# Feed-forward tiles finished inside attention, one tile stored instead of two; value sums multiplied with their reciprocals by GpSimd

## The chip, the cores and the metric

The kernel runs on one core of a Trainium2 chip. The metric is the device time of one execution in microseconds; a kernel's time is the median of its runs. TensorE multiplies matrices (PE; its weight loads are PEld), VectorE (DVE), ScalarE (ACT) and GpSimd (POOL) work element by element, and SyncE (SP) issues most of the DMAs. Each engine takes its own instructions in order; engines wait for each other through semaphores. TensorE writes to PSUM, of which the kernel uses eight tiles of 128 x 512: two each of the names pa, pb, ps1 and ps2.

## What is computed

Sequence S = 2048, width D = 512, 32 heads of 16, window W = 256, feed-forward width F = 1792, all in float32:

```python
qkv = (x @ wqkv) ...                            # 32 heads
scores = einsum("bhqd,bhkd->bhqk", q, k) * Dh ** -0.5
mask = (i - j >= 0) & (i - j < W)
a = (softmax(where(mask, scores, -1e9)) @ v) @ wo
b = (silu(x @ w_gate) * (x @ w_up)) @ w_down
g = sigmoid((x * gate_w).sum(-1))
out = g * a + (1 - g) * b
```

## The kernel before

Every float32 operand of a product is split in a high part (cast to the multiplication's type) and a low part (the rest), and a product is the sum of three: high x high, high x low, low x high. `split` does it with one cast and one subtraction.

The kernel has three stages. In preparation the inputs are split and the first two groups of heads are projected. In attention, heads go in 8 groups g of 4, and a group takes 16 **steps** t of four **blocks** hd. A block issues one score product of the next group, of which VectorE takes the row maximum (`stage1`: scores into ps1, then an add of the mask and a reduction in one operation, with its accumulator read), and one score product of this group, transposed, of which ScalarE takes the exponential (`stage2`: scores into ps2, then `pt`); GpSimd zeroes what lies outside the window. Every fourth step, behind block 1, `av` multiplies the exponentials with the values into one tile pb and one ps2 (pa and ps1 at the end). `finish` adds the two on VectorE, transposes, takes reciprocals of the sums (`rc`), multiplies, transposes back, and stores to `od`; its pieces are spread over the four steps that follow, at the blocks that the main loop names.

Into the same blocks go other products, three pairs of matmuls in each: the projections of the groups 2 to 7, key `("p", g)`, and the feed-forward products x @ w_gate and x @ w_up of 13 of the 14 tiles f of 128 columns, keys `("f", f, 0)` and `("f", f, 1)`. `lanes` computes two 512-column chunks m at a time, each on half of the array's rows, in two **turns** of 12 yields (one step each): in the second turn the chunks swap row halves. Since the two halves of one sum must not be accumulated at once, the first matmul of the second turn waits for an instruction of the list `BEHIND` (exponentials in the order in which they are issued; in preparation also score reductions): the first one recorded after the last matmul of the first turn was issued (`mark`).

`unit(key, t)` takes a whole key in four steps, with the two halves hf of the sequence interleaved: turn 0 of hf 0 in pa, turn 0 of hf 1 in pb, turn 1 of hf 0, turn 1 of hf 1. A step or two later ScalarE copies the finished tiles to `ev` tiles in SBUF (five of them in a ring, `kept`). Feed-forward tiles are stored to DRAM (`raws`, gate and up apart), projections are split and rearranged (`stack`).

`prepare` splits the weights of a coming key and starts the load of the next. In the last group, tiles of w_down are loaded, and the output gate is computed.

In the feed-forward stage, `load_kept` brings a gate tile and an up tile back per (f, c), `hidden` takes Silu of the gate tile on ScalarE and multiplies on VectorE, `halved` splits, and `step` multiplies with w_down (L85 to L87). Tile f = 13 is computed there whole (L700). The attention output is multiplied with wo beside it, and `put` mixes and stores. `tile0` does the first tile's Silu and product at the border of the stages.

Of the kernel before, what the change touches and what calls it, by code (L numbers as in the profile page):

```python
# [16 lines left out]
P = 128  # L17
S, D, H, DH, W, F = 2048, 512, 32, 16, 256, 1792
NK = D // P
NB = S // P  # L20
# [13 lines left out]
def gated_mix(ctx, tc, xT, xn, wqk, wv, wo, wgu, wd, gw, out):  # L34
# [103 lines left out]
    early = [("f", f, i) for f in range(NF - 1) for i in range(2)]  # L138
    KEPT = {(f, i, c) for _, f, i in early for c in range(NCH)}
    UNITS = []  # L140
# [8 lines left out]

    WKEYS = list(UNITS)  # L150
    WKEYS += [("f", NF - 1, i) for i in range(2)]
# [22 lines left out]
    with ExitStack() as A:  # L174
# [151 lines left out]
        def av(g, c):  # L326


            AV[g, c] = (pp.tile([P, CH], F32, name="pb" if 4 * g + c + 1 < len(UNITS) else "pa"),
                        ps1.tile([P, CH], F32, name="ps1") if 4 * g + c + 1 >= 4 * (G - 1) else ps2.tile([P, CH], F32, name="ps2"))  # L330

            orders = [[4 * c + m for m in ms if 4 * c + m >= 0] for ms in ((0, 1, 2, -1, -2, 3), (0, 1, -1, 2, 3, -2))]
            for n, kbs in enumerate(zip(*orders)):
                for j in range(4):
                    for h, (o, kb) in enumerate(zip(HALVES, kbs)):
                        k0 = kb * P + 64 * h
                        q0, q1 = max(k0, c * CH), min(k0 + W + 64, c * CH + CH)
                        nc.tensor.matmul(AV[g, c][h][32 * j:32 * j + 32, q0 - c * CH:q1 - c * CH],  # L338
                                         VG[4 * g + kb // 4][o, kb % 4, 17 * j:17 * j + 32],
                                         PT[g, kb, j // 2][o, j % 2, q0 - kb * P:q1 - kb * P],  # L340
                                         start=n == 0, stop=n == len(orders[0]) - 1, skip_group_check=True)
# [3 lines left out]
        def finish(g, c):  # L345
# [18 lines left out]
            nc.vector.tensor_tensor(out=v[:, :, :DH], in0=v[:, :, :DH],  # L364
# [147 lines left out]
        def unit(key, t):  # L512


            later(t, 3, prepare)

            def done(hf):
                def copies(ps):
                    t0 = t + 3 + hf
                    places = [kept(), kept()]  # L520
                    for m in range(2):
                        later(t0, 2 * m if t0 < G * NB else 0, lambda m=m: nc.scalar.copy(places[m], ps[m]))  # L522
                    if key[0] == "f":
                        for m in range(2):
                            later(t0 + 1, 2, lambda m=m: nc.sync.dma_start(raws[key[1], key[2], 2 * hf + m], places[m]))
                        return
                    g = key[1]

                    def half(m):
                        if m == 0:  # L530
                            X[g, hf] = x_pair()
                        split_qk(g, hf, m, places[m])
                    t1 = t0 + 3 * hf
                    later(t1, 3, lambda: half(0))
                    later(t1 + 1, 1, lambda: half(1))
                    later(t1 + 1, 3, lambda: stack(g, hf))
                return copies
# [43 lines left out]
        def tile0_load():  # L581
            for i, place in enumerate(halves_of(halves_of(KT[1][1])[0])):
                GOT[ORDER[0], i, 0] = place.bitcast(F32)
                nc.sync.dma_start(GOT[ORDER[0], i, 0], raws[ORDER[0], i, 0])

        def tile0():
            (gt, up), sg = [GOT.pop((ORDER[0], i, 0)) for i in range(2)], kept()
            nc.scalar.activation(sg, gt, AF.Silu)
            nc.vector.tensor_tensor(out=sg, in0=up, in1=sg, op=ALU.mult)
            split(*TILE0, sg, nc.scalar, nc.vector)  # L590
# [7 lines left out]
        for t in range(G * NB + 1):  # L598
            g, i = divmod(t, NB)
            d, part = divmod(t, NSLOT)  # L600
            if part == 0:
                turns = unit(UNITS[d], t) if d < len(UNITS) else [iter(())] * NSLOT
            s1 = stage1(g + 1, i) if t < g7 else iter(())
            s2 = stage2(g, i) if t < G * NB else iter(())
            for hd in range(4):
# [5 lines left out]
                run(turns[part], 3)  # L611
# [20 lines left out]
    with ExitStack() as B:  # L632
        hp = B.enter_context(tc.tile_pool(name="hp", bufs=3, side="right"))
        got = B.enter_context(tc.tile_pool(name="got", bufs=4, side="right"))
# [50 lines left out]
        def load_kept(c, f):  # L685

            for i in range(2):
                GOT[f, i, c] = got.tile([P, CH], F32, name=f"got{i}")
                nc.sync.dma_start(GOT[f, i, c], raws[f, i, c])

        def hidden(c, f):
            gu = []
            for i, name in enumerate(("pa", "pb")):
                if (f, i, c) in KEPT:
                    gu.append(GOT.pop((f, i, c)))
                    continue
# [6 lines left out]
            nc.scalar.activation(sg, gu[0], AF.Silu)  # L703
            nc.vector.tensor_tensor(out=sg, in0=gu[1], in1=sg, op=ALU.mult)  # L704
# [46 lines left out]
        for _ in range(3):  # L751
# [65 lines left out]
```

## Time and profile before

| | |
|---|---|
| median of 3 runs | 822.22 us (821.8 to 822.39) |
| the profiled execution | span 821.5 us from its first to its last instruction |
| mean granted TensorE clock | 1.000 |
| HBM read, written | 61.08 MB, 45.61 MB |
| 104 stores `raws`, 102 + 2 loads of it | 256 KB each |
| 512 exponentials (L316) | 477 ns each |
| 512 score reductions (L277) | 539 ns each, and 140 for the accumulator's read |
| 128 copies of `ev` (L522) | 587 ns each |

The profiled execution's own time is its span; the span is 0.7 us under the median of the runs. In the lines quoted below, L12 is line 12 of the kernel before. A row of a timeline gives start and length in us, engine, line, operation, output <- inputs with shapes, how many of them, and in brackets the idle time of the engine before it and what ended it. A row of a group gives the busy time in all and the mean of one in ns after the first bar, and after the second the idle time before it and its releasers.

### The profile page before, as it was taken

What the parts mean: (1) busy time and instruction counts of PE and PEld (TensorE: products, weight loads), DVE (VectorE), ACT (ScalarE), POOL (GpSimd) and SP (SyncE); (2) the same over time, 40 slices, a digit from 0 to 9 for tenths busy, and PEclk for the clock granted to TensorE, in tenths of its full rate; (3) what the DMA queues carried; (4) which work ended last, traced back from release to release, by engine and by line L of the source; (5) the groups of instructions that cost most, each with busy time, mean ns of one, the idle gap of its engine ahead of it and who ended that gap; (6) DMA issues with size and microseconds to landing.
All of it is one profiled execution on the core that took longest, in us unless ns stands there. A gap on an engine that the chain in (4) does not pass through costs nothing.

```text
span 821.5 us, 21573 instructions
## 1 busy us (share of the span) xinstructions
PE 815.1 (99%) x8329; PEld 683.8 (83%) x8329; DVE 515.6 (63%) x1437; ACT 448.9 (55%) x936; POOL 351.8 (43%) x640
## 2 busy tenths in 40 slices
PE   8999999999999999999999999999999999999998
PEld 7888988888888888888888888888887888888886
DVE  6397677677667676677677667756567453443543
ACT  6422666666656666666666666656654433333341
POOL 7812555555546555645554655456511221011020
PEclk9999999999999999999999999999999999999999
DMA  8574534624534543552562463466698563383531
GB/s 294 164 206 150 154 121 125 191 94 146 166 128 125 161 146 117 152 170 101 144 193 102 126 191 125 160 207 201 210 325 267 182 197 110 131 244 107 178 125 51
DMA packets 67957, 133.26 MB, mean 162 GB/s; under 512 B 11600, under 2 KB 16336, under 8 KB 67856
## 3 DMA queue, kind: packets, MB, share of 16 engines
q1 hardware_dynamic: 63888, 118.00, 46.3%
q0 software_dynamic: 3968, 13.90, 4.6%
q8 instruction: 65, 1.06, 0.6%
q14 instruction: 36, 0.29, 0.1%
HBM read 61.08 MB, written 45.61 MB: 130 GB/s over the span
## 4 chain that ended last, share of the span: by engine, by line
PE 95%; DMA 2%; DVE 1%; ACT 1%; issue 1%; SPq 0%; DVEq 0%; ACTq 0%
PE pb L225 24%; PE pa L225 24%; PE pb L338 7%; PE ps L275 6%; PE ps L87 5%; PE ps L85 5%; PE ps L86 5%; PE ps L314 5%; PE pb L205 2%; PE pa L205 2%; PE pb L85 2%; PE pb L87 2%; PE pb L86 2%; PE ps L338 2%; DMA got<-raws 1%; PE pb L700 1%
## 5 line engine op out<-in xcount | busy, mean ns | idle before, releaser
L277 DVE CUSTOM_DVE_ANT_0 ps<-ps,mask 128x384 f32<-128x384 f32 (+2 forms) x512 | 271.6, 539 | 143.2 <-PE ps L314 66.7
L316 ACT ACTIVATE pt<-ps 128x384 f32<-128x384 f32 (+2 forms) x512 | 240.7, 477 | 114.9 <-PE ps L275 57.7
L318 POOL TENSOR_SCALAR_AFFINE_SELECT pt<-pt 128x256 f32<-128x256 f32 x256 | 107.4, 419 | 223.8 <-ACT pt L316 220.4
L314 PE MATMUL ps<-q,k 64*128 64x384 f32 (+2 forms) x512 | 159.9, 329 | 0.0
L275 PE MATMUL ps<-k,q 63*128 63x384 f32 (+2 forms) x512 | 158.7, 330 | 0.0
L225 PE MATMUL pb<-xhi,wh 64*128 64x512 f32 x512 | 111.3, 394 | 0.0
L225 PE MATMUL pb<-xlo,wh 64*128 64x512 f32 x512 | 110.1, 391 | 0.0
L225 PE MATMUL pb<-xhi,wl 64*128 64x512 f32 x512 | 109.9, 392 | 0.0
L225 PE MATMUL pa<-xhi,wh 64*128 64x512 f32 x512 | 109.0, 394 | 0.0
L225 PE MATMUL pa<-xhi,wl 64*128 64x512 f32 x512 | 107.9, 391 | 0.0
L225 PE MATMUL pa<-xlo,wh 64*128 64x512 f32 x512 | 107.8, 391 | 0.0
L275 PEld LDWEIGHTS ps<-k,q 63*128 63x128 f32 x512 | 88.8, 185 | 16.9 <-issue 5.7
L321 POOL TENSOR_SCALAR_AFFINE_SELECT pt<-pt 128x256 f32<-128x256 f32 x224 | 98.7, 441 | 0.0
L314 PEld LDWEIGHTS ps<-q,k 64*128 64x128 f32 x512 | 89.9, 184 | 5.4 <-issue 0.8
L704 DVE TENSOR_TENSOR sg<-got,sg 128x512 f32<-128x512 f32 x51 | 45.1, 885 | 64.6 <-ACT sg L703 59.9
L338 PE MATMUL ps<-pt,vg 64*32 64x320 f32 (+4 forms) x1408 | 75.0, 346 | 0.0
L338 PE MATMUL pb<-pt,vg 64*32 64x320 f32 (+3 forms) x1360 | 73.9, 350 | 0.0
L277 DVE DVE_READ_ACCUMULATOR2_ANT mx<- 128x1 f32 x512 | 71.9, 140 | 0.0
L338 PEld LDWEIGHTS pb<-pt,vg 64*32 64x32 f32 x1360 | 46.4, 106 | 28.3 <-ACT pt L316 9.9
L225 PEld LDWEIGHTS pb<-xhi,wh 64*128 64x128 f32 x512 | 56.6, 185 | 7.9 <-ACT ev L522 0.3
L225 PEld LDWEIGHTS pb<-xhi,wl 64*128 64x128 f32 x512 | 56.5, 184 | 6.7
L225 PEld LDWEIGHTS pa<-xhi,wl 64*128 64x128 f32 x512 | 54.7, 184 | 7.4
(159 smaller groups left out, 1576.6 us busy)
## 6 DMA issues: line engine op xcount, KB each, us to landing
raws<-ev SPq DMA_DIRECT2D x104, 256.0 KB
got<-raws SPq DMA_DIRECT2D x102, 256.0 KB
od<-o POOLq DMA_DIRECT2D x32, 256.0 KB, 2.6
raw<-wgu SPq DMA_DIRECT2D x28, 256.0 KB
q<-xhi SPq DMA_DIRECT2D x56, 128.0 KB
k<-xhi SPq DMA_DIRECT2D x56, 128.0 KB
vd<-vs POOLq DMA_DIRECT2D x8, 672.0 KB, 5.1
vg<-vd SPq DMA_DIRECT2D x32, 168.0 KB
```

What stands on the lines that cost most here:

```text
L85: nc.tensor.matmul(ps, lh, rh, start=start and i == 0, stop=False, skip_group_check=skip)
L86: nc.tensor.matmul(ps, lh, rl, start=False, stop=False, skip_group_check=skip)
L87: nc.tensor.matmul(ps, ll, rh, start=False, stop=stop and i == n - 1, skip_group_check=skip)
L225: mm = nc.tensor.matmul(ps[me], w[r], x[r], start=not second and i == 0, stop=bool(second) and i == n - 1)
L275: nc.tensor.matmul(ps[:, :n], QT[g % 2][pr][r, q0:q0 + P], KT[g % 2][pr][r, k0:k0 + n], start=True, stop=True)
L277: mx = nc.vector.tensor_tensor_reduce(out=ps[:, :n], in0=ps[:, :n], in1=mask[:, 3 * P - n:], scale=1.0, scalar=NEG, op0=ALU.add, op1=ALU.m ...
L314: nc.tensor.matmul(ps[:, :n], KT[g % 2][pr][r, k0:k0 + P], QT[g % 2][pr][r, k0:k0 + n], start=True, stop=True)
L316: BEHIND.append(nc.scalar.activation(pt[:, j, :n], ps[:, :n], AF.Exp, scale=SCALE))
L318: nc.gpsimd.affine_select(out=pt[:, :, :P], in_=pt[:, :, :P], pattern=[[0, 2], [1, P]], compare_op=ALU.is_ge, fill=0.0, base=0, channel_mu ...
L321: nc.gpsimd.affine_select(out=pt[:, :, 2 * P:], in_=pt[:, :, 2 * P:], pattern=[[0, 2], [-1, P]], compare_op=ALU.is_ge, fill=0.0, base=-1, ...
L338: nc.tensor.matmul(AV[g, c][h][32 * j:32 * j + 32, q0 - c * CH:q1 - c * CH], VG[4 * g + kb // 4][o, kb % 4, 17 * j:17 * j + 32], PT[g, kb, ...
L704: nc.vector.tensor_tensor(out=sg, in0=gu[1], in1=sg, op=ALU.mult)
```

## The change

Instead of whole keys in four steps, `TURNS` lists pairs (key, half of the sequence), and `unit(n)` takes one pair in two steps: turn 0, then turn 1, in pa for even n and pb for odd n. For each tile f and half hf the gate product comes first (pa) and the up product next (pb). When the gate sum is done, ScalarE takes tanh of its half into an `ev` tile and VectorE multiplies (tanh + 1) with the sum; when the up sum is done, VectorE multiplies with one half and with the sum. That is silu(gate) x up, since silu(z) = z (1 + tanh(z / 2)) / 2. One tile per (f, chunk) is stored (`kept_h`), and the feed-forward stage only loads and splits it; the tile f = 13 uses the same formula there. Weights are prepared two steps ahead of a key's first turn. In `finish`, the product with the reciprocals is done by GpSimd. The pool of loaded tiles has eight places of one tile instead of four places of two names, and six loads are issued ahead instead of three pairs.

```diff
+    KEPT = {(f, c) for f in range(NF - 1) for c in range(NCH)}
+    tiles = iter([[(("f", f, i), hf) for i in range(2)] for f in range(NF - 1) for hf in range(2)])
+    TURNS = []
     for g in range(2, G):
-        UNITS += early[:2] + [("p", g)] + early[2:3]
-        early = early[3:]
-    UNITS += early
-    raws = dram.tile([NF - 1, 2, NCH, P, CH], F32, name="raws")
+        for n in range(4):
+            TURNS += [(("p", g), hf) for hf in range(2)] if n == 2 - g % 2 else next(tiles)
+    for two in tiles:
+        TURNS += two
...
+    kept_h = dram.tile([NF - 1, NCH, P, CH], F32, name="kept_h")
...
             nc.vector.reciprocal(rc, v[:, :, DH])
-            nc.vector.tensor_tensor(out=v[:, :, :DH], in0=v[:, :, :DH],
+            nc.gpsimd.tensor_tensor(out=v[:, :, :DH], in0=v[:, :, :DH],
                                     in1=rc[:, :, None].to_broadcast([P, CH // 32, DH]), op=ALU.mult)
...
-        def unit(key, t):
-            later(t, 3, prepare)
...
-            (a0, a1), (b0, b1) = (lanes(pp, name, [products(key, 2 * hf + m) for m in range(2)], done(hf))
-                                  for hf, name in enumerate(("pa", "pb")))
-            return [a0, b0, a1, b1]
+        for key in KEYS[1:-1]:
+            later(FIRST[key] - 2, 1, prepare)
...
+        def gate_half(t, f, hf):
+            def done(ps):
+                def tanh(m):
+                    SIL[f, hf, m] = kept()
+                    nc.scalar.activation(SIL[f, hf, m], ps[m], AF.Tanh, scale=0.5)
+                def product(m):
+                    nc.vector.scalar_tensor_tensor(SIL[f, hf, m], SIL[f, hf, m], 1.0, ps[m], op0=ALU.add, op1=ALU.mult)
+                for m in range(2):
+                    later(t + 2 + m, 0, lambda m=m: tanh(m))
+                    later(t + 2 + m, 3 - m, lambda m=m: product(m))
+            return done
+        def up_half(t, f, hf):
+            def done(ps):
+                hs = [SIL.pop((f, hf, m)) for m in range(2)]
+                def product(m):
+                    nc.vector.scalar_tensor_tensor(hs[m], hs[m], 0.5, ps[m], op0=ALU.mult, op1=ALU.mult)
+                for m in range(2):
+                    later(t + 2, 3 * m if t + 2 < G * NB else 0, lambda m=m: product(m))
+                    later(t + 3, 2, lambda m=m: nc.sync.dma_start(kept_h[f, 2 * hf + m], hs[m]))
+            return done
...
+        def unit(n):
+            t, (key, hf) = 2 * n, TURNS[n]
+            done = group_half(t, key[1], hf) if key[0] == "p" else (gate_half, up_half)[key[2]](t, key[1], hf)
+            return lanes(pp, ("pa", "pb")[n % 2], [products(key, 2 * hf + m) for m in range(2)], done)
...
-            if part == 0:
-                turns = unit(UNITS[d], t) if d < len(UNITS) else [iter(())] * NSLOT
+            if t % 2 == 0:
+                turns = unit(t // 2) if t < G * NB else [iter(())] * 2
...
-                run(turns[part], 3)
+                run(turns[t % 2], 3)
...
         def hidden(c, f):
+            if (f, c) in KEPT:
+                return GOT.pop((f, c))
...
-            nc.scalar.activation(sg, gu[0], AF.Silu)
-            nc.vector.tensor_tensor(out=sg, in0=gu[1], in1=sg, op=ALU.mult)
+            nc.scalar.activation(sg, gu[0], AF.Tanh, scale=0.5)
+            nc.vector.scalar_tensor_tensor(sg, sg, 1.0, gu[0], op0=ALU.add, op1=ALU.mult)
+            nc.vector.scalar_tensor_tensor(sg, sg, 0.5, gu[1], op0=ALU.mult, op1=ALU.mult)
             return sg
```

On TensorE, this is the border of a second turn in the kernel before, in attention; xhi, xlo, wh and wl are the high and low parts of x and of a weight tile, and what a row waits for stands in brackets (Activation is ScalarE):

```order
L225 MATMUL pa<-xlo_72,wh 128x512
L225 MATMUL pa<-xhi_73,wl 128x512
L225 MATMUL pa<-xhi_71,wl 128x512
L275 MATMUL ps_2440<-k_92,q_90 128x384 [waits DVE_49]
L314 MATMUL ps_2444<-q_358,k_360 128x384 [waits Activation_49]
L225 MATMUL pb<-xhi_77,wh 128x512
L225 MATMUL pb<-xhi_75,wh 128x512
L225 MATMUL pb<-xlo_78,wh 128x512
```

And the border of a second turn in the changed kernel:

```order
L229 MATMUL pa<-xlo_78,wh 128x512
L229 MATMUL pa<-xhi_75,wl 128x512
L229 MATMUL pa<-xhi_77,wl 128x512
L279 MATMUL ps_2308<-k_92,q_90 128x256 [waits DVE_49]
L318 MATMUL ps_2312<-q_358,k_360 128x384 [waits Activation_49]
L229 MATMUL pa<-xhi_77,wh 128x512 [waits Activation_49]
L229 MATMUL pa<-xhi_75,wh 128x512
L229 MATMUL pa<-xlo_78,wh 128x512
```

Before, the turn ahead is that of another tile (pa, then pb), and the second turn's first row waits for nothing. Now the same tile pa goes on, and its first row waits for ScalarE; by `mark` that is the exponential of the scores in the row just ahead (L318).

On VectorE, this is the last step of four and the first of the next in the kernel before, up to the sum of the value products (L355); `mx` rows are the score reductions with their accumulators' reads:

```order
L367 STREAM_TRANSPOSE o_1342<-o_1341 128x512
L277 ISA ps_2470,mx<-ps_2470,mask 128x384 [waits PE_49]
L277 ISA mx 128x1
L277 ISA ps_2484,mx<-ps_2484,mask 128x384 [waits PE_49]
L277 ISA mx 128x1
L277 ISA ps_2500,mx<-ps_2500,mask 128x384 [waits PE_49]
L277 ISA mx 128x1
L277 ISA ps_2516,mx<-ps_2516,mask 128x384 [waits PE_49]
L277 ISA mx 128x1
```

And the same place in the changed kernel, up to the up product (L541) that empties the tile pb which the value products take next:

```order
L371 STREAM_TRANSPOSE o_1342<-o_1341 128x512 [waits Pool_49]
L281 ISA ps_2466,mx<-ps_2466,mask 128x384 [waits PE_49]
L281 ISA mx 128x1
L529 SCALAR_TENSOR_TENSOR ev<-ev,pa 128x512 [waits DMAHW5_49,Activation_49]
L281 ISA ps_2480,mx<-ps_2480,mask 128x384 [waits PE_49]
L281 ISA mx 128x1
L281 ISA ps_2494,mx<-ps_2494,mask 128x384 [waits PE_49]
L281 ISA mx 128x1
L541 SCALAR_TENSOR_TENSOR ev<-ev,pb 128x512
```

Two products with PSUM operands stand among the reductions, and the transpose now waits for GpSimd. Ahead of these rows stands the reduction of the same block as the transpose.

More of the change, by code (lines that the diff above doesn't have):

```diff
@@ new lines, in group_half, with done, half @@
+        def group_half(t, g, hf):
+            t0 = t + 2 + (not hf)
+            def done(ps):
+                places = [kept(), kept()]
+                for m in range(2):
+                    later(t0, 2 * m, lambda m=m: nc.scalar.copy(places[m], ps[m]))
+                def half(m):
+                    if m == 0:
+                        X[g, hf] = x_pair()
+                    split_qk(g, hf, m, places[m])
+                first = t0 + 3 * hf
+                later(first, 3, lambda: half(0))
+                later(first + 1, 1, lambda: half(1))
+                later(max(first + 1, (g - 1) * NB) if hf else first + 1, 3, lambda: stack(g, hf))
+            return done
@@ L581, in tile0_load @@
         def tile0_load():
-            for i, place in enumerate(halves_of(halves_of(KT[1][1])[0])):
-                GOT[ORDER[0], i, 0] = place.bitcast(F32)
-                nc.sync.dma_start(GOT[ORDER[0], i, 0], raws[ORDER[0], i, 0])
+            GOT[ORDER[0], 0] = halves_of(halves_of(KT[1][1])[0])[0].bitcast(F32)
+            nc.sync.dma_start(GOT[ORDER[0], 0], kept_h[ORDER[0], 0])
         def tile0():
[L587 to L590, printed above, removed]
+            split(*TILE0, GOT.pop((ORDER[0], 0)), nc.scalar, nc.vector)
         later(g7 + NB - 4, 1, tile0_load)
@@ L633, in gated_mix @@
         hp = B.enter_context(tc.tile_pool(name="hp", bufs=3, side="right"))
[L634 removed]
+        got = B.enter_context(tc.tile_pool(name="got", bufs=8, side="right"))
         bp = B.enter_context(tc.tile_pool(name="bp", bufs=2))
@@ L750, in gated_mix @@
         loads = [(c, ORDER[n]) for c, n in seq if n != 1 and c + n]
-        for _ in range(3):
+        for _ in range(6):
             load_kept(*loads.pop(0))
```

41 lines of the change are left out of this document (9 added, 32 removed).

## The prediction

> **What bounds the kernel now.** I read the page's head and its busy times first, then the chain of work that ended last, then the windows by stage, and last the timeline of one stretch.
>
> ```profile
> span 821.5 us, 21573 instructions
> ...
> PE 815.1 (99%) x8329; PEld 683.8 (83%) x8329; DVE 515.6 (63%) x1437; ACT 448.9 (55%) x936; POOL 351.8 (43%) x640
> ...
> PE 95%; DMA 2%; DVE 1%; ACT 1%; issue 1%; SPq 0%; DVEq 0%; ACTq 0%
> ```
>
> TensorE is busy for 815.1 of 821.5 us and holds 95% of the chain. Nobody else sets the end: VectorE works 63% of the span, ScalarE 55%, GpSimd 43%. The stages are read one by one (columns: stretch, its length, then busy time of PE, PEld, DVE, ACT, POOL, granted clock, DMA share, GB/s): preparation up to 80.7, the 128 steps of attention up to 598, the feed-forward stage after it. The last row, from a finer answer, is the very end.
>
> ```profile
> 0.00:80.70 80.70, 78.53 (x530) 64.52 (x532) 52.39 (x155) 32.25 (x57) 40.34 (x50) 1.00 0.68 207
> 80.70:598.00 517.30, 517.25 (x6799) 438.36 (x6804) 357.32 (x1136) 330.25 (x730) 282.92 (x568) 1.00 0.48 151
> 598.00:821.50 223.50, 219.33 (x1019) 180.95 (x1003) 105.91 (x146) 86.44 (x151) 28.54 (x22) 1.00 0.54 173
> ```
>
> ```profile
> 815.00:821.50 6.50, 2.68 (x15) 2.17 (x13) 2.35 (x4) 0.00 (x0) 0.00 (x0) 0.96 0.43 161
> ```
>
> Preparation, with 2.17 us of standing, is not touched by the change. In attention TensorE is shown standing for 0.05 us; VectorE is busy 357 of 517 us. In the feed-forward stage TensorE stands 4.17 us, and 3.82 of these lie at the very end, behind the last products and the store. So whatever is taken off VectorE, ScalarE or the queues is worth under a microsecond, and whatever makes TensorE wait costs its full length. The question is only whether the change makes it wait.
>
> **The wait that the change adds.** Two chunks of a product are summed side by side, each on half of the array's rows, and swap the halves after the first of two turns; the first matmul of the second turn waits for the first exponential (or score reduction) recorded after the first turn's end. Before, another tile's turn stood between the two, so four exponentials had passed; the second turn's first row carries no wait. Now the second turn follows directly, and the exponential it must wait for is the one whose scores stand in the row just ahead of it (first pair of fences in the section on the change). 64 units of two turns make 64 such waits. Matmuls start in order, so all of TensorE's work stands behind each: the turn's 24 products, the next scores, and through them ScalarE and VectorE. What one wait costs is read from the same place in the trace of before:
>
> ```profile
> 301.19 0.34 PE L275 MATMUL ps<-k,q 63*128 63x384 f32 x1
> ...
> 301.20 0.33 PE L314 MATMUL ps<-q,k 64*128 64x384 f32 x1
> 301.37 0.39 PE L225 MATMUL pa<-xhi,wh 64*128 64x512 f32 x2
> ...
> 301.60 0.49 ACT L316 ACTIVATE pt<-ps 128x384 f32<-128x384 f32 x1 [0.37 <-PE ps L314]
> ...
> 303.80 0.33 PE L314 MATMUL ps<-q,k 64*128 64x384 f32 x1
> ...
> 303.97 0.40 PE L225 MATMUL pb<-xhi,wh 64*128 64x512 f32 x2
> ...
> 304.27 0.49 ACT L316 ACTIVATE pt<-ps 128x384 f32<-128x384 f32 x1 [0.37 <-PE ps L275]
> ```
>
> From the scores' start to the exponential's end it is 301.60 + 0.49 - 301.20 = 0.89 us in one block and 304.27 + 0.49 - 303.80 = 0.96 in the other, on average 0.93. The turn's products started 0.17 after the scores, and now start after the 0.93. The restart has a price too:
>
> ```profile
> 623.27 0.68 DVE L70 TENSOR_TENSOR hl<-sg,hh 128x512 fp32r<-128x512 f32 x1
> ...
> 623.71 0.39 PE L86 MATMUL ps<-k,hh 128*128 128x512 f32 x1
> ...
> 624.00 0.19 PEld L87 LDWEIGHTS ps<-k,hl 128*128 128x128 f32 x1 [0.32 <-DVE hl L70]
> 624.00 0.50 PE L87 MATMUL ps<-k,hl 128*128 128x512 f32 x1
> ```
>
> This matmul waited for VectorE, whose write ended at 623.95; it starts 0.05 later, its weight load has waited with it, and it lasts 0.50 instead of the 0.39 of its neighbour. So 0.03 to wake (between nothing and 0.05) and 0.11 for the uncovered load: one wait costs 0.93 + 0.03 + 0.11 - 0.17 = **0.90 us**. Bounds: 0.89 - 0.17 = 0.72 with neither, 0.96 + 0.05 + 0.11 - 0.17 = 0.95 with all. Times 64: **57.6 us** (46.1 to 60.8). In the last eight units two scores go out ahead of the turn and the wait is for the first exponential, so I leave them at the same price.
>
> A page bears on the 0.11. The Trainium skill (TensorE: Matmul & The Clock Gate, Part 2, step 1) says that TensorE pulls a weight load ahead of matmuls in flight. By that the load would be over when the wait ends, and the sum would be 64 x 0.11 = 7 us less, some 875 us. The row at 624.00 speaks against it where the matmul waits on a semaphore: there the load waited too.
>
> **The other parts.** TensorE's matmuls are the same in number and size, in another order. Of the rest, these rows carry the prices (line, engine, operation | busy in all, mean ns):
>
> ```profile
> L70 POOL TENSOR_TENSOR wl<-raw,wh 128x512 fp32r<-128x512 f32 (+2 forms) x36 | 46.1, 1281 | 3.2 <-ACT wh L67 3.2
> L704 DVE TENSOR_TENSOR sg<-got,sg 128x512 f32<-128x512 f32 x51 | 45.1, 885 | 64.6 <-ACT sg L703 59.9 <-DMA got<-raws 4.7
> ...
> L522 ACT COPY ev<-pb 128x512 f32<-128x512 f32 x64 | 37.7, 590 | 0.5 <-PE pb L225 0.5
> ...
> L703 ACT ACTIVATE sg<-got 128x512 f32<-128x512 f32 x51 | 32.1, 629 | 4.6 <-DMA got<-raws 3.6 <-DVE hl L70 1.0
> ...
> L364 DVE TENSOR_TENSOR o<-o,rc 128x256 f32<-128x256 f32 x32 | 16.4, 511 | 1.1
> ...
> L675 DVE SCALAR_TENSOR_TENSOR k<-ps,igate,k 128x512 f32<-128x512 f32 x8 | 5.4, 742 | 0.0
> ...
> L588 ACT ACT_TABLE_LOAD x1 | 1.3, 1283 | 0.0
> ```
>
> And the transfers, from the page's list of DMA issues:
>
> ```profile
> raws<-ev SPq DMA_DIRECT2D x104, 256.0 KB
> got<-raws SPq DMA_DIRECT2D x102, 256.0 KB
> ```
>
> - Feed-forward stage: 51 Silu (32.1 us), 51 products (45.1 us), half of the 102 loads and one table load leave ScalarE, VectorE and the queues. TensorE's matmuls cover them all; only its own stands ahead of the end can go: 4.17 - 3.82 = 0.35, and the 0.32 at 624.00, which the busy time hides. I take -0.6 us (0 to -0.7). The one tile loaded goes straight to the split; with up to eight in flight it is not late where two tiles of each pair were not.
> - ScalarE in attention: 104 of the copies (0.59 each) go, 52 tanh come, for which the Silu row's 0.63 is nearest. Its load falls by 61 - 33 = 28 us; nothing waits longer.
> - GpSimd: 32 value products. Below, VectorE's 0.51; above, GpSimd's 1.28 for twice the elements, and half of it is 0.64, which I take. The next user, VectorE's second transpose, stands a whole step (four blocks) later, some 3.5 us, and the one long job that may stand ahead on GpSimd is a 1.28 us weight split: covered, 0 us. Without that cover each would delay VectorE by up to 1.3 us.
> - The halved stores and the weights' splits, now two steps apart instead of four, stay off the path: a split takes 0.6 + 1.3 us and its load waits behind nothing longer, against 2 x 3.5 us.
> - VectorE in attention gains 104 scalar-tensor-tensor products at 0.74 (77 us) and loses 16.4. On average it has room (357 of 517 us, then some 418 of 575), but it works in order, and the value sums need an accumulator that its up-product frees.
>
> The last is the second place at which TensorE can wait. The spacing of VectorE's jobs when they queue:
>
> ```profile
> 301.03 0.55 DVE L277 CUSTOM_DVE_ANT_0 ps<-ps,mask 128x384 f32<-128x384 f32 x1
> ...
> 301.56 0.57 DVE L277 CUSTOM_DVE_ANT_0 ps<-ps,mask 128x384 f32<-128x384 f32 x1
> ...
> 303.79 0.71 DVE L367 STREAM_TRANSPOSE o<-o 128x512 f32<-128x512 f32 x1
> ...
> 304.42 0.54 DVE L277 CUSTOM_DVE_ANT_0 ps<-ps,mask 128x384 f32<-128x384 f32 x1
> ...
> 306.87 0.51 ACT L316 ACTIVATE pt<-ps 128x384 f32<-128x384 f32 x1
> ...
> 307.05 0.40 PE L225 MATMUL pa<-xhi,wl 64*128 64x512 f32 x2
> ...
> 307.38 0.10 PEld L338 LDWEIGHTS pb<-pt,vg 64*32 64x32 f32 x1 [0.37 <-ACT pt L316]
> ```
>
> A reduction follows the one before after 0.53, a job follows a transpose after 0.63; a product of mean 0.74 I put at 0.67. Count from the start of the last step of four, whose block 0 now has the 0.90 wait; a block is 0.87 (three of them lie between the scores at 301.20 and those at 303.80). Block 1's scores start at 1.77 and reach VectorE 0.37 later (301.19 to 301.56), at 2.14. Then come in its order, up to the product that frees the accumulator, four reductions, a transpose and two products (second pair of fences): 4 x 0.53 + 0.63 + 2 x 0.67 = 4.09, end 6.23, some 0.07 for the write: 6.30. TensorE reaches the value sums after six blocks and the wait, 6 x 0.87 + 0.90 = 6.12. In the trace of before it waits there already, for an exponential that ends at 307.38; the last pair of products began at 307.05 and such pairs follow each other after 0.23, so that wait is worth 0.1. So 0.1 us more at 26 places: **3 us**; bounds 0, and 0.5 x 26 = 13 if the jobs take their whole 0.57, 0.71 and 0.74.
>
> **Sum:** 821.5 + 57.6 + 3 - 0.6 = 881.5 us for the profiled execution. The median of the runs, 822.22, lies 0.7 above its span, so the forecast is **882 us**. From the bounds: 822.2 + 46.1 + 0 - 0.7 = 868 to 822.2 + 60.8 + 13 - 0 = 896.
>
> **Rivals.**
> 1. *No wait, so not slower.* If the exponential named is one that is over already, as before, 822.2 - 0.6 = **821.6 us** is left, and the small gain counts as none. It turns on one point: whether at least one more block of products stands between the exponential's scores and the waiting matmul (0.93 of latency against a block of 0.87 brings the wait to about 0.1). The rows show none between them. Chance 0.04.
> 2. *VectorE becomes the bound of a round.* If its products run as slowly as the 885 ns of the row of L704, and GpSimd's product lands late besides, both tanh products and the accumulator come late: the chain above grows by some 0.2 x 2 for the products and 1.3 for the transpose, and 26 x 1.7 = 44 us come on top of 879: **923 us**; half of it 901. For it: VectorE is the next engine in load. Against: the 0.74 row reads PSUM as these do, and each wait lets VectorE catch up 0.9. Chance 0.06 for more than 896.
> 3. *The clock falls because TensorE stands often.* What the trace has of short idles:
>
> ```profile
> 8.00:10.00 2.00, 1.51 (x6) 0.86 (x6) 1.40 (x3) 1.80 (x3) 0.00 (x0) 1.00 0.92 197
> ```
>
> With 0.49 us idle in 2 us the granted clock stays 1.00; only behind the last 3.8 us it is 0.96. At 0.96 over attention's 517 us, 517 x 0.04 = 21 us come on top: **903 us**. Chance 0.03. The Trainium skill (TensorE: Matmul & The Clock Gate, Part 1, on PSUM-queue cycling) reports a kernel whose short idles between groups made the clock swing to half; 64 swings of one 3.4 us window would be 64 x 1.7 = 109 us by that page, an estimate, and some 990. The row at 8.00, with its idles at full clock, does not bear it out.
>
> **How the numbers follow.** Forecast 0.84 (within 866 to 896), and 0.03 for a smaller loss than the bounds allow; the rivals as given. The range 866 to 896 leaves out 0.16. A measurement of this kernel tells about 0.2% (1.6 us) from no change. Slower: 0.84 + 0.03 + 0.06 + 0.03 = 0.96; same 0.03 and faster 0.01, both out of rival 1.
>
> **What would show it.** In the profile after: TensorE's busy time stays near 815 while the span grows, or its weight loads show idle of some 0.5 to 0.8 us, 64 times, released by ScalarE's exponential at the turns' line; two steps of attention last 0.9 us longer; the clock row stays at 1.00; the feed-forward stage from its first matmul to the end is as long as before within 1 us; VectorE's idle behind scores grows. Wrong if these waits are absent or under 0.5 us each, if value sums wait for VectorE over 0.5 us each, or if the stage after attention changes by several us.

## The result and the profile after

The changed kernel takes 887.74 us, 1.0795 times the kernel before [1.0777, 1.0812]. One of its four executions, the profiled one, took 1682.09 us with a TensorE that was slow from preparation on, where the change does nothing (226 matmuls in the first 80.7 us, 530 before), while the others took 887.21 to 888.1. Measured a second time beside the first experiments it took 887.78 us; the profile below is from there, and its span lies 65.3 us above that of before (886.8 - 821.5). This is the head of the page after, with the chain of work that ended last:

```profile
span 886.8 us, 21259 instructions
...
PE 836.0 (94%) x8329; PEld 677.7 (76%) x8329; DVE 519.2 (59%) x1461; ACT 401.5 (45%) x831; POOL 362.7 (41%) x672
...
PE 90%; DVE 4%; ACT 4%; DMA 1%; issue 1%; SPq 0%; POOL 0%; DVEq 0%; ACTq 0%
```

TensorE has the same 8329 matmuls, but now it stands for 50.8 us of the span, where it stood 6.4 before, and each restart lengthens its busy time besides. ScalarE and VectorE, which had 1% of the chain each, have 4%. By stages (the same columns as before, the borders moved to the same places of the program):

```profile
0.00:80.70 80.70, 78.66 (x532) 65.20 (x534) 52.33 (x157) 32.57 (x58) 39.57 (x51) 1.00 0.66 207
80.70:664.20 583.50, 538.64 (x6797) 431.50 (x6801) 392.86 (x1207) 312.43 (x678) 295.54 (x600) 0.99 0.35 110
664.20:886.80 222.60, 218.73 (x1018) 180.98 (x995) 74.00 (x100) 56.48 (x96) 27.59 (x23) 1.00 0.36 114
```

All of the loss lies in attention: 583.5 us for the same work as 517.3, with the DMA share down from 0.48 to 0.35 and ScalarE's busy time down by 18 us. None of what was saved there is seen in the time. What TensorE and its weight loads waited for (us in total, times, longest):

```profile
PE pa L229 <- ACT pt L320: 19.3, 32, 0.6
PE pb L229 <- ACT pt L320: 17.8, 32, 0.7
PE pb L342 <- DVE ev L541: 6.3, 8, 2.1
PE pa L229 <- DVE ev L529: 1.4, 2, 1.3
...
PEld pa L229 <- ACT pt L320: 30.7, 32, 1.0
PEld pb L229 <- ACT pt L320: 29.8, 32, 1.1
PEld pb L342 <- DVE ev L541: 15.9, 24, 2.6
```

The 64 waits at the turns' line are there, released by the exponential, and 24 waits of the value sums for VectorE's up product. In the kernel before, the rows for PE hold none of these, and the value sums' weight loads wait for ScalarE:

```profile
PEld pb L338 <- ACT pt L316: 9.9, 27, 0.4
```

One of the 64 waits, in the timeline of the changed kernel:

```profile
328.93 0.33 PE L318 MATMUL ps<-q,k 64*128 64x384 f32 x1
...
329.35 0.49 ACT L320 ACTIVATE pt<-ps 128x384 f32<-128x384 f32 x1 [0.39 <-PE ps L279]
...
329.89 0.19 PEld L229 LDWEIGHTS pb<-xhi,wh 64*128 64x128 f32 x2 [1.00 <-ACT pt L320]
329.89 0.50 PE L229 MATMUL pb<-xhi,wh 64*128 64x512 f32 x2 [0.61 <-ACT pt L320]
...
330.23 0.40 PE L229 MATMUL pb<-xlo,wh 64*128 64x512 f32 x2
...
330.46 0.40 PE L229 MATMUL pb<-xhi,wl 64*128 64x512 f32 x2
```

The exponential ends 329.35 + 0.49 - 328.93 = 0.91 after its scores' start, the turn begins 0.05 later and not 0.17 after the scores, and the next pair of products follows after 0.34 and not after 0.23: 0.91 + 0.05 - 0.17 + 0.11 = 0.90 us. The weight load waited with its matmul, so the 0.11 is paid; the pull-ahead of which the Trainium skill speaks (TensorE: Matmul & The Clock Gate, Part 2, step 1) does not help here.

Where the 65.3 us lie is read from a marker. Near the end of the next to last group SP sends its last row of maxima (`q<-md`), behind 56 of the 64 second turns; the first matmul of the feed-forward stage ends attention. For the kernel before:

```profile
538.25 0.99 SPq L293 DMA_DIRECT2D q<-md  x2
...
L700 PE MATMUL pa<-xhi,wh x16: 389/389/497, 598.9 to 762.4; 128*128 128x512 f32 x16
```

For the changed kernel:

```profile
592.50 0.98 SPq L297 DMA_DIRECT2D q<-md  x2
...
L724 PE MATMUL pa<-xhi,wh x16: 389/389/496, 665.0 to 827.7; 128*128 128x512 f32 x16
```

Up to the marker 54.2 us are lost, in the last group 72.5 - 60.7 = 11.8, and the feed-forward stage, from its first matmul to the end, falls from 222.6 to 221.8 us.

### The profile page after: what moved, and what is told of

It is laid out like the page before. It is cut to its first block, busy times and chain, and to the rows that moved or that the text cites. A ratio compares the mean times of both kernels' runs of the same rounds, so it can differ in the third digit from the quotient of the medians.

```text
span 1680.3 us, 21259 instructions
## 1 busy us (share of the span) xinstructions
PE 1637.9 (97%) x8329; PEld 1069.0 (64%) x8329; DVE 534.3 (32%) x1461; ACT 408.2 (24%) x831; POOL 359.6 (21%) x672
## 2 busy tenths in 40 slices
DMA packets 52979, 105.97 MB, mean 63 GB/s; under 512 B 9936, under 2 KB 14672, under 8 KB 52880
## 4 chain that ended last, share of the span: by engine, by line
PE 98%; ACT 2%; issue 0%; DVE 0%; POOL 0%; DVEq 0%; POOLq 0%; ACTq 0%
PE pb L229 24%; PE pa L229 24%; PE ps L279 7%; PE ps L85 6%; PE ps L87 6%; PE ps L86 6%; PE pb L342 5%; PE ps L318 3%; PE ps L342 3%; PE pb L209 2%; PE pa L209 2%; PE pb L86 2%; ACT pt L320 2%; PE pb L87 2%; PE pb L85 2%; PE pa L724 1%
## 5 line engine op out<-in xcount | busy, mean ns | idle before, releaser
L279 PE MATMUL ps<-k,q 63*128 63x384 f32 (+2 forms) x512 | 251.6, 525 | 0.0
L318 PE MATMUL ps<-q,k 64*128 64x384 f32 (+2 forms) x512 | 250.2, 521 | 0.0
L229 PE MATMUL pb<-xhi,wh 64*128 64x512 f32 x512 | 181.5, 679 | 17.9 <-ACT pt L320 17.9
L229 PE MATMUL pa<-xhi,wh 64*128 64x512 f32 x512 | 179.9, 676 | 19.2 <-ACT pt L320 19.2
L229 PE MATMUL pb<-xhi,wl 64*128 64x512 f32 x512 | 181.9, 679 | 0.0
L229 PE MATMUL pa<-xhi,wl 64*128 64x512 f32 x512 | 180.2, 676 | 0.0
L229 PE MATMUL pa<-xlo,wh 64*128 64x512 f32 x512 | 180.1, 674 | 0.0
L229 PE MATMUL pb<-xlo,wh 64*128 64x512 f32 x512 | 179.8, 670 | 0.0
L318 PEld LDWEIGHTS ps<-q,k 64*128 64x128 f32 x512 | 143.0, 295 | 25.0 <-issue 12.9
L342 PE MATMUL pb<-pt,vg 64*32 64x320 f32 (+3 forms) x1360 | 142.1, 606 | 0.0
L229 PEld LDWEIGHTS pa<-xhi,wh 64*128 64x128 f32 x512 | 75.7, 277 | 70.9 <-ACT pt L320 42.7
```

What stands on the lines that cost most here:

```text
L229: mm = nc.tensor.matmul(ps[me], w[r], x[r], start=not second and i == 0, stop=bool(second) and i == n - 1)
L279: nc.tensor.matmul(ps[:, :n], QT[g % 2][pr][r, q0:q0 + P], KT[g % 2][pr][r, k0:k0 + n], start=True, stop=True)
L318: nc.tensor.matmul(ps[:, :n], KT[g % 2][pr][r, k0:k0 + P], QT[g % 2][pr][r, k0:k0 + n], start=True, stop=True)
```

## The experiments

Each was timed beside the kernel before, on the same chip as it (the kernel before took 822.1 to 822.4 us each time). Three theories were open. A: each second turn waits for an exponential just issued. B: products that stand on VectorE return PSUM tiles late, since its queue is in order. C: GpSimd's product, or another part of the change, costs time too.

**1. The changed kernel again.**

> The changed kernel once more, for a profile of a run that is not disturbed. Theory A (the second turn's wait): 64 waits of TensorE's weight loads for the exponential, 0.5 to 0.8 us of recorded idle each, 885 to 890 us in all, and the feed-forward stage as long as before. Theory B (VectorE's added load and order): the largest waits of TensorE are for VectorE, spread over all blocks. Theory C (GpSimd's product is late): VectorE's second transposes wait for GpSimd, over 1 us each.

887.78 us (ratio 1.0786 [1.077, 1.0803]); its profile is the one above.

**2. The kernel before, with the order of the turns alone.**

```diff
-            return [a0, b0, a1, b1]
+            return [a0, a1, b0, b1]
```

> The kernel before with one line changed: the four turns of a key in the order pa, pa, pb, pb instead of pa, pb, pa, pb. Nothing else of the change is in it. Theory A: 64 waits of 0.9 us, 822.3 + 57 = 879 us (868 to 884). Theory B and theory C: 822 us, since VectorE and GpSimd do what they did.

882.21 us (ratio 1.0727 [1.0712, 1.0742]): 59.8 us, 0.93 for each of the 64 waits. One line of order, which removes and adds no instruction, makes nine tenths of the loss. Its weight loads' waits at the turns:

```profile
PEld pa L225 <- ACT pt L316: 35.8, 32, 1.2
PEld pb L225 <- ACT pt L316: 30.3, 32, 1.1
```

**3. The changed kernel, with gate and up turns interleaved** over four steps as before, and everything that hangs on their ends moved along; only the core is shown.

```diff
+                turns = list(two) if part == 0 else [turns[0], two[0], turns[1], two[1]]
...
-                    later(t + 2, 3 * m if t + 2 < G * NB else 0, lambda m=m: product(m))
+                    later(t + 4, 3 * m if t + 4 < G * NB else 0, lambda m=m: product(m))
```

> The changed kernel with its gate and up turns interleaved again (gate, up, gate, up over four steps), and the evacuations and the pieces of the value sums' finish moved to fit; all operations are the changed kernel's. Theory A: the 64 waits are gone and 821 to 828 us are left. Theory B: still over 870 us. Theory C: still over 870 us, since GpSimd multiplies as in the changed kernel.

853.75 us (ratio 1.0378 [1.0364, 1.0392]), so A's expectation, 821 to 828, missed by over 25 us, and those of B and C, over 870, by over 16. The 64 waits are gone, but others have come:

```profile
PEld pb L229 <- DVE ev L542: 14.6, 25, 0.9
...
PEld pb L342 <- DVE ev L542: 13.3, 24, 1.5
...
PEld pa L229 <- DVE ev L530: 7.4, 5, 2.4
```

The timeline shows how: the product that frees a tile pb stands in VectorE's queue behind a reduction and the value sums' adding, and the next turn in pb is due before it has ended.

```profile
202.66 0.68 DVE L359 TENSOR_TENSOR o<-pb,o 128x512 f32<-128x512 f32 x1
...
203.27 0.56 DVE L281 CUSTOM_DVE_ANT_0 ps<-ps,mask 128x384 f32<-128x384 f32 x1
...
203.74 0.68 DVE L542 SCALAR_TENSOR_TENSOR ev<-ev,pb 128x512 f32<-128x512 f32 x1
...
204.47 0.49 PE L229 MATMUL pb<-xhi,wh 64*128 64x512 f32 x1 [0.36 <-DVE ev L542]
```

**4. The kernel before, with GpSimd's product alone.**

```diff
-            nc.vector.tensor_tensor(out=v[:, :, :DH], in0=v[:, :, :DH],
+            nc.gpsimd.tensor_tensor(out=v[:, :, :DH], in0=v[:, :, :DH],
```

> The kernel before with only the value sums' product moved to GpSimd. Theory A: within 1 us of 822.3. Theory B: the same or up to 1 us less. Theory C: slower by tens of us, and VectorE's second transposes wait for GpSimd.

822.23 us (ratio 0.9999 [0.999, 1.0008]). VectorE waits for it (`DVE o L367 <- POOL o L364`, 6.1 us at five places), and TensorE does not. For the product, C falls.

**5. Half the dose of the second run.**

```diff
-            return [a0, b0, a1, b1]
+            return [a0, a1, b0, b1] if t % 8 == 0 else [a0, b0, a1, b1]
```

> The kernel before, with the second turns put straight behind the first ones in every other unit of four steps only (32 of the 64 pairs); nothing else of the change. A (each of these turns waits for the exponential whose scores stand in the row just ahead, at a fixed price): half of the 59.8 us that all 64 cost, so 822.4 + 29.9 = 852.3 us, 850.5 to 854.5, and some 66 / 2 = 33 us of weight-load waits for the exponential at the turns, 32 times. Rival (the waits are a matter of the stage's balance: ScalarE or VectorE fall behind once for all, and recover where the order is loose): clearly other than half, below 845 or above 860 us.

852.99 us (ratio 1.0372 [1.0355, 1.0389]): 30.8 us for 32 waits, 0.96 each. The loss goes with the number of waits, as A says.

**6 and 7. The third run, with the products on VectorE one place earlier:** first the up products alone, then the gate's tanh and products too.

```diff
-                    later(t + 4, 3 * m if t + 4 < G * NB else 0, lambda m=m: product(m))
+                    later(t + 3 + m, 3 - 3 * m, lambda m=m: product(m))
```

```diff
-                    later(t + 3, m, lambda m=m: tanh(m))
-                    later(t + 3, m + 1, lambda m=m: product(m))
+                    later(t + 2 + m, 3 - 3 * m, lambda m=m: tanh(m))
+                    later(t + 3, m, lambda m=m: product(m))
```

> The changed kernel with its turns interleaved as before (853.75 us), and only the two products of each up pair moved ahead by one place: to the end of the step in which its second turn ends, and to the start of the next. B (the 31 us by which that kernel stands over the kernel before come from PSUM tiles that VectorE gives back one step too late, behind the value sums' adding in its queue): the waits of pb's turns and of the value sums for these products go, 14.6 and 13.3 us of weight-load waits, of which some 10 come back as the wait for the exponential that the kernel before has too; with the restarts 829 to 834 us, the gate products' 7 us still there. Rival (VectorE's whole load, or the clock, makes the 31 us): no more than 5 us go, 848 us or above.

> As the run with the up products moved, and the gate's tanh and products moved ahead by one place too (a tanh at the end of the step of the gate's second turn, the products in the two places behind). A with B: no turn waits for an exponential just issued, no PSUM tile comes back late, so the kernel before less the 0.9 us of the feed-forward stage: 821.5 us, 820 to 825. That would put all of the change's loss on the order in which the turns stand and the places at which products stand, and nothing on fewer stores, more GpSimd or the finished tiles themselves. Rival (VectorE's added work costs time wherever it stands): 828 us or above.

835.44 us (ratio 1.0162 [1.0146, 1.0177]) and 833.96 (1.0144 [1.0125, 1.0162]). The up products of 26 pairs at another place of the same queue take 18.3 us away (the expectation, 829 to 834, is missed by 1.4), which bears out B and not VectorE's load. But the second of the two was expected at 821.5, and 12 us were still there: it is only 1.5 us below the first, and their intervals overlap. TensorE's waits for gate products (7.7 us in the sixth run) are gone in it, but its value sums wait 7.5 us for up products, which they did not in the sixth. By the same marker, 542.72 and 611.0, 4.5 of the 12 lie ahead of the last group and 7.6 in it. There VectorE and TensorE of the seventh run show:

```profile
554.60 2.53 DVE L586 SCALAR_TENSOR_TENSOR xhi<-xlo,xhi 128x512 f32<-128x512 f32 x1
...
557.38 0.43 DVE L69 CAST q<-ev 128x512 fp32r<-128x512 f32 x1 [0.24 <-DMA ev<-wd]
...
559.05 1.28 DVE L542 SCALAR_TENSOR_TENSOR ev<-ev,pb 128x512 f32<-128x512 f32 x2
```

```profile
559.79 0.45 PE L342 MATMUL pb<-pt,vg 64*32 64x320 f32 x1 [3.40 <-DVE ev L542]
```

The up products stand behind the output gate's blocks of xn (L586) and the pieces of w_down (L69). The row of L586 shows no wait for a transfer: it lasts 2.53 us, where the middle one of its 16 lasts 0.76, and why is not shown. It does not set the time, though. The chain that ended last (start, length, what) goes back to w_down's transfer, which SP issued behind its fetch of xn (L583); and that fetch waits for VectorE to be done with an earlier block:

```profile
551.74 0.56 DVE xhi L586 x2
...
552.32 0.33 SPq L583
...
552.70 4.65 DMA ev<-wd
...
557.38 0.44 DVE q L69
...
559.14 0.61 DVE ev L542
```

Other blocks of xn do wait for their own transfers, 5.6 us at two places. The kernel before has such waits of VectorE there too (8.3 us for xn at four places in its trace, 3.7 for w_down), but its copies out of PSUM stood on ScalarE. That is a new theory, D: the change put a reader of PSUM into a queue that waits for DMAs.

**8. The changed kernel, with the up products one place earlier.**

```diff
-                    later(t + 2, 3 * m if t + 2 < G * NB else 0, lambda m=m: product(m))
+                    later(t + 1 + m, 3 - 3 * m, lambda m=m: product(m))
```

> The changed kernel with the two products of each up pair one place earlier, nothing else; its 64 second turns still wait for the exponential. A with B: the value sums' 15.9 us of waits for these products go, and some 10 us come back as the wait for the exponential that the kernel before has there; 887.8 less 6 (4 to 8) = 882 us, 880 to 884, as the kernel before with this order of the turns alone (882.2). Rival (the 5.6 us between these two come from VectorE's load, or from the clock's fall late in the last group): 886 us or above, or the granted clock between 620 and 640 us as low as in the changed kernel.

883.43 us (ratio 1.0748 [1.0726, 1.0769]), 4.35 us less, within the expectation. Its marker stands at 587.74, 4.8 ahead of the changed kernel's: that is what late up products cost the value sums up to the last group. TensorE's seven waits for them there, 4.1 us, are gone, and the granted clock is 1.00 up to the marker in both. The 56 waits that are left cost 587.74 - 538.25 = 49.5, or 0.88 each. In the last group it is still 9.8 us over the kernel before, of which 8 x 0.88 = 7.0 are waits; the value sums' longest wait for L541, 2.2 us, is there, and so is a granted clock of 0.83 between 618 and 628 us. So the rival's lower clock is there too, with up products early or late, but it lies behind the marker and doesn't make the 4.8.

**9 and 12. The seventh run, with more time for the transfers:** in the ninth for xn and w_down, in the twelfth for xn alone (the edit of the first fence).

```diff
-            t = g7 - 4 + b // 2 * 2
+            t = g7 - 4 + b
...
-            later(t + 1, 2 + b % 2, lambda b=b: gate_block(b))
+            later(t + 2, 0, lambda b=b: gate_block(b))
```

```diff
-            later(t, 2, lambda: later(t + 1, 2, load_wd(f, piece, kept())))
+            later(t, 2, lambda: later(t + 2, 1, load_wd(f, piece, kept())))
```

> The run with interleaved turns and all products early (833.96 us), and in the last group the transfers that VectorE waits for get more time: the blocks of xn one a step and multiplied seven places after their fetch instead of five, the pieces of wd split seven places after theirs instead of four. D (what is left of the loss, 12 us ahead of the feed-forward stage, comes from VectorE waiting in its queue for xn and wd while the up products and with them the value sums of TensorE stand behind; 7.5 us of waits at four places and a clock of 0.83 for 10 us after the longest): most of it goes, 824 us, 822 to 828, and the granted clock between 550 and 610 us is 1.00 throughout. Rival (the transfers only come later, since SP issues them no earlier, or the waits move to other engines): 831 us or above.

> The run with interleaved turns and all products early (833.96 us), with the blocks of xn one a step and their longer lead, and nothing else: the pieces of wd and the weights at their old places. It parts the two transfers that VectorE waits for. If xn's alone hold TensorE up: 826 to 828 us, the last stage again 222.3 us from its first matmul to the end; if wd's alone do: 833 to 835 us; if both: between, some 830 us. It also says what moving the weights by one place did in the run before this (836.23 us, where six value sums wait 9.1 us for a copy behind it): if that was the whole of it, this run is below 832 us.

827.96 us (ratio 1.007 [1.0056, 1.0084]) and 827.76 (1.0074 [1.0061, 1.0087]): 6 us of the 12 go, so 827.96 lies at the edge of what was expected (824, 822 to 828), and the granted clock of the ninth is 1.00 as expected. In the twelfth run attention ends at 604.0 instead of 611.0, 6.3 of these 7 behind the marker (542.00). That bears out D, and moving xn's blocks alone is enough; but it doesn't part the two transfers, since both stand in SP's queue and the edit moves VectorE's blocks too. From 540 us on, VectorE waits 5.6 us for xn and 2.4 for w_down in the seventh run, and 0 and 7.7 in the twelfth. So the waits for transfers are no shorter in sum, only the value sums wait less behind them. Part of the 6 us is the clock, which falls to 0.63 for 4 us in the seventh run (last section) and stays at 1.00 in the twelfth. In the ninth attention ends at 602.2, but the late split of the last pieces makes the feed-forward stage 224.2 us instead of 222.3 (826.4 and 833.3 less the first matmul's time). The waits of the value sums for L542, 7.5 us in the seventh run (four, the longest 3.4), are gone in the ninth; in the twelfth they are

```profile
PE pb L342 <- DVE ev L542: 2.3, 3, 1.1
```

**10. The seventh run, with the value product on VectorE again** (the edit of the fourth run undone).

> The run with interleaved turns and all products early (833.96 us), and the value sums multiplied with their reciprocals by VectorE again. D: VectorE waits for transfers as before, so no change, 833 to 835 us. Rival (GpSimd's product costs after all once products stand on VectorE: VectorE's 3.8 us of waits for it in the last group, and the masks that stand in GpSimd's queue behind a product that waits 3.6 us for its reciprocals): 830 us or below.

836.51 us (ratio 1.0175 [1.0158, 1.0192]), 2.6 us more than the seventh run where no change was expected; the intervals just touch. GpSimd's product costs nothing here either, and where VectorE's queue holds TensorE up it seems to save a little.

**11. The twelfth run, with the weights split one place earlier.**

```diff
-            later(t if key[0] == "f" and key[2] else t - 1, 1, prepare)
+            later(t if key[0] == "f" and key[2] else t - 1, 0, prepare)
```

> Interleaved turns, all products early, the blocks of xn one a step with their longer lead as in the run before this (827.96 us), but the pieces of wd split at their old places, since the late split of the last ones made the feed-forward stage 2 us longer there (224.2 us from its first matmul to the end, against 222.3); and the weights split one place earlier, since seven turns wait 0.4 us for a weight half by GpSimd. D: the 222.3 us come back, the weights give up to 1 us, 825 us, 822 to 827; what the wd pieces' waits cost in VectorE's queue shows as 0 to 3 us more in the last group. Even at best this is the kernel before within 0.4 us, because fewer stores and GpSimd's product bring TensorE nothing. Rival (the finished tiles save something that the waits have hidden so far): below 820 us.

836.23 us (ratio 1.0162 [1.0144, 1.0179]), 8.5 us more than without the edit, where up to 1 us less was expected. The profiled execution, at a clock of 1.000, is 5.4 us longer than the twelfth run's (831.9 and 826.5); three of the five show a clock of 0.996 to 0.998 and are some 3 us longer still. The waits say why the 5.4:

```profile
PE pb L342 <- ACT ev L555: 9.1, 6, 2.2
```

In the timeline, the longest of the six:

```profile
446.45 0.62 ACT L67 CAST wh<-raw 128x512 fp32r<-128x512 f32 x1 [2.02 <-DMA raw<-wgu]
446.98 0.58 ACT L555 COPY ev<-pb 128x512 f32<-128x512 f32 x1
...
447.61 0.45 PE L342 MATMUL pb<-pt,vg 64*32 64x320 f32 x1 [2.23 <-ACT ev L555]
```

It is D on another engine: the weight split, moved ahead, waits 2.02 us in ScalarE's queue for its transfer, a projection's copy out of PSUM (L555) stands behind it, and the value sums wait for that tile. The rival, a saving that the waits had hidden, is not seen in any run: none is measurably below the kernel before.

## Why the prediction was right, and where its sizes were off

It forecast 882 us (866 to 896); measured were 887.74. Its own steps:

1. *What bounds the kernel.* That only what makes TensorE wait counts was borne out from both sides: 27 MB less traffic (133.26 to 105.97 in the pages' totals) and 47 us less work for ScalarE (448.9 to 401.5) bought 0.8 us at most (step 5), and one line of order cost 59.8 us.
2. *64 waits for the exponential just ahead, 0.90 us each, 57.6 us.* Right, in place, number and size: 0.90 in the timeline above, 0.93 and 0.96 by the doses in the kernel before, whose ScalarE has copies besides, and 0.88 by the marker of the eighth run, so some 56 us of the changed kernel's 65.
3. *VectorE's order makes value sums wait 0.1 us at 26 places, 3 us (0 to 13).* The mechanism was right, 24 places by the profile; the size was too small. The eighth run puts the part up to the last group at 4.8 us, 0.2 a place. One of its signs of being wrong was met, value sums that wait over 0.5 us each for VectorE: their weight loads wait 0.66 (15.9 us at 24 places). But in the kernel before they waited 0.37 for the exponential already (9.9 us at 27), so the change adds less than that sign counts.
4. *What the sum lacked* lies in the last group: 11.8 us lost there, against 7.0 of turn waits. The reading of VectorE's queue was made for a group with score reductions, and the last group has waits for transfers in it instead, for xn ahead of a gate product and for w_down ahead of an up product:

```profile
623.06 0.69 DVE L585 SCALAR_TENSOR_TENSOR xhi<-xlo,xhi 128x512 f32<-128x512 f32 x1 [2.64 <-DMA xlo<-xn]
...
624.42 0.49 PE L229 MATMUL pa<-xhi,wh 64*128 64x512 f32 x1 [1.25 <-DVE ev L529]
...
625.26 0.95 DVE L69 CAST q<-ev 128x512 fp32r<-128x512 f32 x1 [0.90 <-DMA ev<-wd]
...
627.46 0.68 DVE L541 SCALAR_TENSOR_TENSOR ev<-ev,pb 128x512 f32<-128x512 f32 x1
...
628.20 0.74 PE L342 MATMUL pb<-pt,vg 64*32 64x320 f32 x1 [2.14 <-DVE ev L541]
```

   Two standstills of 1.25 and 2.14 us, and behind them a lower clock (below). The four runs of this kernel have mean clocks of 1.000, 0.998, 0.996 and 0.996 and spans of 884.2, 885.4, 886.5 and 886.8, so by these four the clock makes some 2.6 of the 4.8 us that are left, and late products the other 2.2; both are estimates.
5. *The feed-forward stage, -0.6 us.* Measured -0.8. *ScalarE, stores, weight splits, GpSimd: 0.* Right by the fourth run for GpSimd, whose product took 0.62 us where 0.64 was taken; it is not covered everywhere (VectorE's second transposes wait 4.8 us for it, at five places), but TensorE does not wait there. For the others, TensorE shows no wait in the changed kernel. The loads were read less well: in attention ScalarE's busy time fell by 17.8 us and not 28, and VectorE's grew by 35.5 and not some 61; no term of the sum hangs on them.

Added up: 49.5 + 4.8 up to the marker, 7.0 + 2.6 + 2.2 in the last group, -0.8 behind it, 65.3 us. Since single executions of one kernel lie up to 4 us apart (the eighth run's spans go from 880.0 to 884.4), the smaller terms are good to 2 us or so.

The rivals: with no wait, 821.6, was refuted by the waits themselves. VectorE as the bound of every round did not come; its products took 0.68 us and not 0.885. The clock's fall over all of attention did not come either; it was confined to one place that the prediction had not named.

**What stays open.** The best order found here, 827.76, is still 5.6 us over the kernel before. 542.00 - 538.25 = 3.8 of them lie ahead of the last group. The weight loads of seven turns wait 0.4 us each for GpSimd's weight halves, but moving these brought the eleventh run's loss, so that cause is argued and not shown. In the last group, which part of D is the transfers and which the order in the queues of VectorE and SP is open too.

## What to carry to other kernels

Where an instruction waits for "the first event recorded after" a point, its price is the distance between that event and itself: two turns next to each other turned a free order into 0.9 us of standstill, and a stream of other work between them is what paid for it. Work moved to a less busy engine also moves into that engine's queue: ask what stands ahead of it there, stage by stage (here transfers in the last group, a sum in the others), and who waits for what it frees. With the bounding engine 99% busy, savings elsewhere were worth under 1 us here, and only new waits counted.

## What was not expected of the hardware

In the changed kernel's trace the granted clock fell at one place, and for a time longer than the standstill. In pieces of 4 us:

```profile
620.00:624.00 4.00, 3.16 (x29) 2.31 (x25) 1.36 (x4) 2.25 (x6) 2.50 (x8) 1.00 0.86 278
624.00:628.00 4.00, 1.65 (x11) 1.04 (x11) 3.07 (x6) 0.34 (x1) 1.93 (x3) 0.90 0.44 153
628.00:632.00 4.00, 3.80 (x80) 1.98 (x81) 0.14 (x1) 0.00 (x0) 0.00 (x0) 0.50 0.62 217
632.00:636.00 4.00, 3.42 (x58) 2.37 (x44) 2.55 (x6) 2.13 (x5) 0.77 (x2) 0.75 0.25 95
```

Behind 4 us with TensorE busy for 1.65, it ran at half clock: the value matmul at 628.20 lasts 0.74, where its like lasts 0.45 in the seventh run. That run shows a fall behind 0.59 of 4 us, and the eighth behind 1.83 of 4 us (0.63 and 0.61 in the next 4). The 64 standstills of 0.6 us never do it, nor do single ones of 2.0 and 2.2 us in the eleventh run's profiled execution, whose clock stays at 1.00. The busy share alone doesn't decide it: that execution has a piece with 1.77 of 4 us (from 444 us) and the seventh run one with 1.91 (from 576), and the clock stays at 1.00 in both and behind both. Nor does the program: executions of the changed kernel have mean clocks from 0.996 to 1.000, and those of the eleventh run too. What decides it is not shown. The Trainium skill (TensorE: Matmul & The Clock Gate, Part 1) tells of a gate that halves the clock after an idle window of some 3.4 us; the half agrees with the row of 628.00. Its rule that no gap should be over some 3.4 us was not enough here: the longest gap ahead of that row was 2.14.
